# Batch 5's 1/rms spread over the partitions by a round trip through DRAM, with a new order of the whole work

## The chip, the core and the metric

The kernel runs on one core of a Trainium2 chip. The metric is the time of one execution on the device in microseconds (us), the median of several runs. The core has five engines, each with its own queue of instructions in a fixed order: TensorE (PE, matmuls, results into PSUM), VectorE (DVE), ScalarE (ACT), GpSimd (POOL) and SyncE (SP). Here GpSimd only issues loads, and SyncE only issues transfers. An instruction that must wait holds up all that is behind it on its engine.

## The reference

```python
# attention: q, k, v are [8 batches, 8 heads, 576, 64]
kv  = einsum('bhsd,bhse->bhde', k, v)
out = einsum('bhsd,bhde->bhse', q, kv)
rms = sqrt(mean(out * out, axis=-1, keepdims=True) + 1e-06)
x   = out / rms * g_norm            # then heads side by side: [8, 576, 512]
# channel mix: w_k [512, 1024], w_v [1024, 512], w_r [512, 512]
x_prev = x shifted by one position, zero first
xk = mu_k * x + (1 - mu_k) * x_prev
xr = mu_r * x + (1 - mu_r) * x_prev
y  = sigmoid(xr @ w_r) * (max(xk @ w_k, 0) ** 2 @ w_v)
```

All inputs and the output are fp32; the kernel computes in bf16 with fp32 sums.

## The kernel before

The attention part goes batch by batch (0 to 7), with channels on the partitions: four pairs of heads of 128 channels each, 576 positions along the free axis. The channel mix goes over nine groups g of 512 positions, across the borders of the batches.

The code defines *pieces* with names, and a string, ORDER, lists all of them by hand. `Plan.run` (L95) walks the string and issues each piece at that place. A token is a name, then the engine if there is a choice (A ScalarE, D VectorE, S SyncE), then the numbers of the buffers that the piece takes: `K5.3::2` takes PSUM slot 2. There are four PSUM slots (`ps`), four output buffers (`out`), two each of k, v, q, qT, uT, xT, and one `sq`. A piece that takes a slot waits on the chip until the last user of that slot is done. So ORDER sets every queue, and the slots set many of the waits.

The pieces of batch b, with their lines:

- `load_kB`, `load_vB`, `load_qB`: loads that turn fp32 into bf16, issued by GpSimd (L280); weights at L264.
- `kv` (L353, L368 for batches 0 and 1): k times v on TensorE, copied out by `kvc` or `kvm`.
- `qT`: q transposed on TensorE (L406, L411, batches 0 to 2), or `qTd` (L394), a transposing transfer on SyncE (batches 3 to 7).
- `u` (L430, L436): q times kv; `uc` copies it to uT, `sq` squares it.
- `st` (L526): sums of squares, all four pairs at once, on TensorE. `rs` (L531): 1/rms on ScalarE, 16 equal rows per head.
- Then 1/rms has to reach all 64 channels of a head. For batches under SPREAD (L145) `sp` (L565, two halves of four matmuls) spreads it into two PSUM slots, and four multiplies `x` (L570) read it there. For the others `rw` (L541) writes one row per head to DRAM, `rr` (L545) reads it back 64 times over into the `sq` buffer, and two multiplies `x` (L550) read that. Batch 0 has its own way (`ss`, `rs`, `x`, L488 to L497).
- `d` (L591): x minus the position before; `tk`, `tr` (L190 or L192): times mu; `xk`, `xr` (L601): the two blends.

The pieces of group g: `K` (L636, eight of them), `relu` (L640) and `sqk` (L643) square the result, `R` (L658) and `sig` (L663) give the gate, `V` (L692) is the second matmul in halves a and b, `o` (L696) multiplies it with the gate into an output buffer, and `S` (L622) stores it, two transfers each. `idle:n` (L742) issues n matmuls on zeros. ScalarE loads a table for 1/sqrt (L204) or sigmoid (at L663) when it goes from one to the other.

In the old order SyncE's queue around the change is: qTd5, S2.0, S2.1, S0.1, S0.0, qTd6, S2.2, S1.3, S2.3, S1.2, qTd7, S3.0, S3.2, rw6, S3.1, rr6, rw7, S4.1, S3.3, rr7, S4.2 and the other stores. ScalarE issues only some of the last stores. o5.1 takes the output buffer that S3.2 and S3.3 store from, and R6.1 the PSUM slot that o5.1 reads.

Of the kernel before, what the change touches and what calls it, by code (L numbers as in the profile page):

```python
# [12 lines left out]


ORDER = """
    zero load_q1.0::0 early_k::0 early_v::1 ident ident9 ones load_v0.6::0 load_q0.6::1 cast_k:D:0 mu_k_load:A load_q0.2
    idle:52:0 qT0.1::0 qT0.3::1 cast_v:A qTc0.3:D:0 load_k0.6 kv0.3::2 qT1.0::3 kv0.0::1 qTc1.0:A:1 kvm0.3::0 kvm0.0 load_q0.0
    qT0.0::2 g_load mu_r_load:S load_q0.4 load_v0.2 sel_load load_k0.4 load_k0.2 mu_mm::3 qT0.2::1 qTc0.0:D qTc0.1:A u0.0::2
    sq0.0::0 u0.3::0 sq0.3 load_v0.4 sel mu uc0.3:A:0 uc0.0:D idle:5:3 ss0.0::3 qTc0.2:A rs0.0::0 kv0.2::2 kv0.1::0 kvm0.2
    kvm0.1 ss0.3::1 u0.2::2 u0.1::0 uc0.2:D load_v1.4::1 load_k1.4::1 load_q1.4 qT1.1::3 load_v1.0 load_k1.0 rs0.3::1 load_w_r0  # L20
    qTc1.1:D x0.0::0 sq0.1 sq0.2 idle:13:1 ss0.2::1 rs0.2::0 ss0.1::3 d0.0::0 tk0.0:D:0 x0.3 d0.3 uc0.1:A rs0.1::1 load_w_r1
    kv1.2::2 idle:2:1 qT1.2::1 kvm1.2::1 qTc1.2:A idle:13:0 u1.2::0 uc1.2:A:1 qT1.3::3 load_w_k0 qTc1.3:A x0.1 tr0.0:D:1 x0.2
    d0.2 d0.1 xr0.0 tr0.1:D tk0.1:D tr0.2:A xr0.2 xr0.1 tk0.2:A idle:9:1 kv1.0::2 tr0.3:D kvm1.0 u1.3::1 uc1.3:A tk0.3:A
    idle:2:0 R0.0::03 R0.1 xr0.3 xk0.0 xk0.1 xk0.3 u1.0::1 uc1.0:D load_w_k1 R0.2 R0.3.1 u1.1::2 sig0.1::0 R0.3.0 sig0.0::1
# [12 lines left out]
    sp3.1::01 V2.1b x3.1.1::1 sp3.0::21 V2.0b x3.1.0 x3.0.0 x3.0.1 V2.2a::0 S0.2 S1.1 S0.3 S1.0 u4.2::21 d3.0::0 d3.2 tk3.0:D:1
    xk3.0 tk3.2:D xk3.2 V2.3a V2.3b uc4.3:A:0 uc4.2:A u4.0::12 sq4.1:A:0 uc4.0:A uc4.1:A V2.2b load_v6.0::1 load_k6.0::0 o2.0::3
    tr3.2:A:0 xr3.2 kv6.0::1 tr3.0:D o2.1::1 K3.3::2 K3.2 kvc6.0.2:A:1 K3.1::3 K3.0 load_k5.0::1 load_v5.0::0 kvc6.0.1:A sq4.0:A
    relu3.1::0 kvc6.0.0:A load_q5.0::1 qTd5::1 st4::0 rs4::0 S2.0 S2.1 S0.1 relu3.0::1 K3.6::2 sp4.0::10 sqk3.1::1 K3.7  # L40
    relu3.3::0 x4.0.1::0 x4.0.0 K3.5::3 load_k7.0::0 kv5.0::0 S0.0 sqk3.0 xr3.0 sp4.1::12 K3.4 x4.1.1 x4.1.0 sqk3.3 relu3.2::1
    sqk3.2 kvc5.0.1:D:0 d4.0::0 R3.3::2 R3.1::1 R3.0 V3.1a::3 V3.1b R3.2 V3.0a V3.0b d4.2 tk4.2:D:1 kvc5.0.0:A kvc5.0.2:A
    tr4.2:A:0 sig3.0::1 tk4.0:D xk4.2 xk4.0 sig3.1::2 load_q7.0::0 K4.6::0 K4.4::1 K4.7 tr4.0:D relu4.3::0 xr4.2 xr4.0 K4.2::2
    K4.5 relu4.2::1 load_q6.0::1 qTd6::0 sqk4.3::0 K4.3 K4.1::0 K4.0 o3.0::3 sqk4.2 relu4.0::0 relu4.1::1 R4.2::1 V3.2a::3 R4.3
    u5.2::02 V3.3a V3.2b sig4.1::0 uc5.2:A:1 uc5.3:D sq5.1:A:0 sqk4.1 sqk4.0 u5.0::12 uc5.0:A V3.3b R4.1::0 uc5.1:D sq5.0:D
    o3.1::2 st5::1 R4.0 rs5::1 sp5.1::23 V4.3a::1 V4.2a x5.1.0::1 x5.1.1 sig4.0::1 load_v7.0::1 sp5.0::23 kv7.0::0 x5.0.1
    d5.2::0 x5.0.0 d5.0 tk5.0:D:1 S2.2 S1.3 S2.3 S1.2 kvc7.0.1:A:0 kvc7.0.2:A tk5.2:A kvc7.0.0:A qTd7::1 V4.2b V4.1a::3 V4.0a
    V4.3b xk5.0 o4.1::1 xk5.2 u6.0::20 V4.0b tr5.0:A:0 uc6.1:A:0 uc6.0:A sq6.0:A:0 S3.0 S3.2 V4.1b u6.2::01 K5.3::2 K5.2 uc6.3:A
    uc6.2:D sq6.1:D st6::1 rs6::0 K5.1::0 relu5.1::1 K5.6::1 K5.7 K5.0 relu5.0::0 tr5.2:D xr5.2 xr5.0 sqk5.1::1 relu5.3::1
    K5.5::2 K5.4 sqk5.0 relu5.2::0 o4.0::0 R5.0::0 R5.1 R5.3::1 V5.3a::2 R5.2 sig5.0::2 sig5.1::0 sqk5.2 sqk5.3 u7.2::30 rw6:S  # L50
    S3.1 rr6:S x6.0::0 x6.1 uc7.2:A:1 uc7.3:A V5.2a V5.3b u7.0::13 V5.1a::0 V5.0a d6.0::0 V5.0b V5.1b V5.2b uc7.1:A sq7.1:A:0
    uc7.0:A sq7.0:A st7::3 rs7::1 rw7:S S4.1 S3.3 rr7:S S4.2 S4.0 d6.2 tk6.0:D:1 tk6.2:D xk6.2 xk6.0 K6.3::1 K6.2 K6.0::3 K6.1
    tr6.2:A:0 relu6.1::0 o5.0::3 tr6.0:D K6.5::0 K6.4 xr6.2 xr6.0 sqk6.1::0 o5.1::2 S5.3 S5.2 relu6.0::1 sqk6.0 K6.6::1 K6.7
    R6.3::3 R6.1::2 relu6.2::0 relu6.3::1 sqk6.3 sqk6.2 R6.0 V6.2a::0 V6.0a::1 V6.0b V6.3a V6.3b R6.2 S5.0 x7.0::1 V6.1a V6.1b
    V6.2b d7.0::0 x7.1 d7.2 tk7.2:D:1 tk7.0:D xk7.0 xk7.2 sig6.1::1 tr7.2:D:0 sig6.0::2 K8.1::3 o6.0::0 o6.1::2 K8.3::2 K8.0
    tr7.0:A relu8.0::1 sqk8.0::1 K8.2 K8.4::1 relu8.1::0 K8.5 K8.6::0 K8.7 S4.3 S6.0 sqk8.1 xr7.2 relu8.2::1 relu8.3::0 sqk8.2
    sqk8.3 V8.3.0a::3 K7.2::2 K7.1::1 K7.3 V8.3.0b K7.0 S6.2 relu7.1::1 K7.4::0 relu7.0::0 K7.6::2 K7.5 K7.7 sqk7.0::0 xr7.0
    relu7.2::0 R8.2::1 R8.3 sqk7.2 relu7.3::0 sig8.1::0 sqk7.1 o8.1.3.0::1 sqk7.3 R7.0::0 R7.1 V8.2a::2 R7.3::1 sig7.0::2 R7.2
    V8.2b V7.2a::3 V7.2b V7.1a::0 o8.1.2.0 S6.3 S8.3.3.0.b:S S8.3.3.0.a:S S5.1 S6.1 S8.2.2.0.a:S sig7.1::1 V7.1b V7.3a V7.3b
    o7.1::2 S7.2.a:A S7.3.a:A R8.1::1 V7.0a V7.0b o7.0::3 V8.1a::2 R8.0 V8.1b S7.3.b:S S7.2.b:A S7.1.a:A V8.0a::3 V8.0b S7.1.b:S  # L60
# [56 lines left out]
def kernel(  # L117
# [15 lines left out]
    B, H, S, HD = q.shape  # L133
# [8 lines left out]
    G = 512  # L142
    NG = B * S // G
    DMA_T = 3
    SPREAD = 6  # L145
    BLOCK = (0,1,)
    DIRECT = ()
    PARTS = {0: ((0, 1), (1, 1), (2, 1), (3, 1)), 1: ((0, 2), (2, 2))}
# [25 lines left out]
             for tag, (n, shape, dt) in BUFS.items() for i in range(n)}  # L174
    scratch = {b: dram.tile([H, S], BF16, name=f"scratch{b}") for b in range(SPREAD, B)}
    plan = Plan()
# [40 lines left out]
    ones = const.tile([128, 2, HD], BF16, name="ones")  # L217
# [3 lines left out]
    sel = const.tile([128, 2, HD], BF16, name="sel")  # L221
# [108 lines left out]
    def attention(b):  # L330
# [183 lines left out]
        else:  # L514
# [21 lines left out]
            xms = {hp: [] for hp in range(NHP)}  # L536
            if b >= SPREAD:
                rows8 = scratch[b]
# [16 lines left out]
                for i in range(2):  # L555
# [219 lines left out]
```

## Time and profile before

| | us |
|---|---|
| median of 9 runs | 207.81 |
| lowest and highest | 206.04, 209.33 |
| the profiled execution | 207.22 |
| its span | 205.2 |

| what, in the profiled execution | start, us |
|---|---|
| first R0 matmul | 23.62 |
| st5, rs5 | 117.50, 117.98 |
| sp5.1, sp5.0 | 118.83, 120.89 |
| x5.1.0 (first x5 multiply), last xk5 ended | 119.16, 127.77 |
| first K5 | 128.13 |
| last V8 matmul ended | 200.52 |

The span runs from the first to the last instruction of the program; the execution's own time has 2.0 us around it. In what follows a line of the profile has the engine, the line of the code, the operation and the tiles (out<-in), and times in us from the start of the span. "x40" counts instructions. In the rows of groups there follow busy time, mean ns of one, and the idle time in front of them with what ended it. In a timeline the first two numbers are start and duration, and a bracket at the end names the idle time before.

### The profile page before, as it was taken

To read this page: it belongs to the slowest core of one execution; us is meant where nothing else is said; L and a number is where in the kernel's file an instruction comes from. 1 tells how busy PE (TensorE), PEld (TensorE's weight loads), DVE (VectorE), ACT (ScalarE), POOL (GpSimd) and SP (SyncE) were. 2 spreads that over 40 slices of the span, in tenths; PEclk is the share of its full clock that TensorE was granted. 3 is DMA by queue.
4 is the path that set the end of the run, shared out by engine and by line. 5 is a ranking of instruction groups with operands and counts; after the bars stand their busy time and mean duration, and the time that the engine had idled before them with its cause. 6 is when DMAs were issued, how large, how long until landed. Compare 5 with 4: busy or idle time off the path is not lost.

```text
span 205.2 us, 3907 instructions
## 1 busy us (share of the span) xinstructions
PE 196.8 (96%) x1578; PEld 98.6 (48%) x1578; DVE 140.2 (68%) x253; ACT 123.0 (60%) x151; POOL 29.7 (14%) x46
## 2 busy tenths in 40 slices
PE   7879999999999999999999999999998999999990
PEld 6858644464344534435476344443443434444440
DVE  3149975999599688989964778869736996241241
ACT  2177877377834586794575879687974256363010
POOL 7984530004000114020200000000000000000000
PEclk9999999999999999999999999999999999999997
DMA  6999999999999599999899991060057414005074
GB/s 156 195 199 202 207 205 205 204 203 204 203 187 216 162 127 132 202 203 177 188 203 218 237 180 40 22 149 0 0 160 242 129 27 127 0 5 143 10 230 128
DMA packets 40437, 30.91 MB, mean 151 GB/s; under 512 B 13644, under 2 KB 35940, under 8 KB 40420
## 3 DMA queue, kind: packets, MB, share of 16 engines
q0 software_dynamic: 21248, 16.48, 52.7%
q1 hardware_dynamic: 18444, 13.14, 26.9%
q10 hardware_dynamic: 728, 1.05, 1.7%
q8 instruction: 12, 0.20, 0.4%
q14 instruction: 5, 0.04, 0.1%
HBM read 34.74 MB, written 9.46 MB: 215 GB/s over the span
## 4 chain that ended last, share of the span: by engine, by line
PE 82%; DMA 5%; DVE 4%; POOL 3%; ACT 2%; issue 1%; SPq 1%; DVEq 0%; POOLq 0%
PE ps L692 29%; PE ps L636 27%; PE ps L658 13%; DMA v<-in_v_dram 3%; PE ps L353 3%; PE ps L436 2%; DMA out_dram<-out 2%; PE ps L742 2%; PE ps L526 1%; POOL q L280 1%; PE ps L565 1%; PE ps L368 1%; POOL k L280 1%; DVE out L696 1%; PE ps L430 1%
## 5 line engine op out<-in xcount | busy, mean ns | idle before, releaser
L692 PE MATMUL ps<-w_v,sqk 128*128 128x512 bf16 (+1 forms) x296 | 67.2, 374 | 0.0
L636 PE MATMUL ps<-xk,w_k 128*128 128x512 bf16 (+1 forms) x320 | 66.0, 358 | 0.3 <-DVE xk L601 0.2
L640 ACT ACTIVATE relu<-ps 128x1024 bf16<-128x1024 f32 x36 | 36.0, 1022 | 28.8 <-PE ps L636 24.1
L636 PEld LDWEIGHTS <-w_k 128*128 128x128 bf16 x320 | 30.1, 98 | 30.9 <-issue 2.3
L692 PEld LDWEIGHTS <-sqk 128*128 128x128 bf16 x296 | 27.7, 98 | 32.9 <-issue 1.8
L643 DVE TENSOR_TENSOR sqk<-relu 128x1024 bf16<-128x1024 bf16 x36 | 24.3, 688 | 20.9 <-ACT relu L640 20.9
L658 PE MATMUL ps<-w_r,xr 128*128 128x512 bf16 x144 | 35.2, 379 | 0.5 <-DVE out L696 0.5
L696 DVE TENSOR_TENSOR out<-ps,sig 128x1024 f32<-128x1024 f32 (+2 forms) x21 | 22.2, 1068 | 16.5 <-PE ps L692 9.5
L663 ACT ACTIVATE sig<-ps 128x1024 bf16<-128x1024 f32 x18 | 18.1, 1022 | 18.5 <-DMA out_dram<-out 9.4
L658 PEld LDWEIGHTS <-xr 128*128 128x128 bf16 x144 | 13.6, 98 | 16.3 <-issue 2.0
L190 ACT ACTIVATE t<-d,mu_sb 128x576 bf16<-128x576 bf16 x23 | 16.5, 770 | 7.5 <-DVE d L591 7.4
L570 DVE TENSOR_TENSOR xT<-uT,ps 128x576 bf16<-128x576 bf16 x20 | 14.2, 750 | 3.3 <-PE ps L565 3.1
L192 DVE TENSOR_SCALAR t<-d,mu_sb 128x576 bf16<-128x576 bf16 x41 | 13.8, 382 | 0.2
L742 PE MATMUL ps<-zeros 128*128 128x224 bf16 x96 | 12.2, 287 | 1.2 <-DVE zeros L231 1.2
L280 POOL DMA_DIRECT2D q<-in_q_dram x12 | 8.6, 720 | 30.4 <-PE ps L411 16.2
L591 DVE TENSOR_TENSOR d<-xT 128x1152 bf16<-128x1152 bf16 (+1 forms) x18 | 12.4, 691 | 0.6
L601 DVE TENSOR_TENSOR xr<-t,xT 128x1152 bf16<-128x1152 bf16 (+1 forms) x18 | 11.8, 684 | 1.5 <-ACT t L190 1.4
L186 DVE CAST uT<-ps 128x576 bf16<-128x576 f32 x12 | 8.8, 753 | 5.5 <-PE ps L436 5.3
L184 ACT CAST uT<-ps 128x576 bf16<-128x576 f32 x16 | 9.8, 636 | 4.5 <-PE ps L436 3.6
L601 DVE TENSOR_TENSOR xk<-t,xT 128x1152 bf16<-128x1152 bf16 (+1 forms) x18 | 11.8, 685 | 0.2
L280 POOL DMA_DIRECT2D v<-in_v_dram x11 | 7.9, 716 | 23.7 <-PE ps L353 22.3
L742 PEld LDWEIGHTS <-zeros 128*128 128x128 bf16 x96 | 9.9, 109 | 2.3 <-DVE zeros L231 1.2
(61 smaller groups left out, 135.5 us busy)
## 6 DMA issues: line engine op xcount, KB each, us to landing
out_dram<-out SPq DMA_DIRECT2D x21, 192.0 KB
v<-in_v_dram POOLq DMA_DIRECT2D x6, 576.0 KB, 10.7
q<-in_q_dram POOLq DMA_DIRECT2D x6, 576.0 KB, 10.5
k<-in_k_dram POOLq DMA_DIRECT2D x6, 576.0 KB, 11.4
out_dram<-out SPq DMA_DIRECT2D x23, 128.0 KB
out_dram<-out SPq DMA_DIRECT2D x21, 64.0 KB
sq<-scratch SPq DMA_DIRECT2D x4, 288.0 KB
w_k<-in_moe_w_k_dram POOLq DMA_DIRECT2D x2, 512.0 KB, 13.0
```

The source lines that it names most:

```text
L190: nc.scalar.mul(out=dst, in_=src, mul=by)
L280: nc.gpsimd.dma_start(out=get(kvq[(n, b)])[:, h0:h1, :], in_=rows(n, b, h0, h1))
L570: nc.vector.tensor_tensor(out=get(xT)[:, 2 * i:2 * i + 2, NP + c:NP + c + HS], in0=flat(slice(2 * i, 2 * i + 2))[:, :, c:c + HS], in1=get( ...
L601: nc.vector.tensor_tensor(out=dst[:, hsl, c0:c0 + S], in0=get(t[key])[:, hsl, :], in1=get(xT)[:, hsl, 0:S], op=ALU.add)
L636: nc.tensor.matmul(get(ps)[:, fc % 2, a0:a1], w_k_sb[:, cc, 128 * fc:128 * fc + 128], xk[:, cc, x0:x0 + a1 - a0], start=(cc == 0), stop=(c ...
L640: nc.scalar.activation(out=get(rt), in_=get(ps), func=AF.Relu)
L643: nc.vector.tensor_mul(out=get(sqk)[:, 2 * f2:2 * f2 + 2, :], in0=get(rt), in1=get(rt))
L658: nc.tensor.matmul(get(ps)[:, ci % 2, :], xr[:, cc, c:c + 128], w_r_sb[:, cc, :], start=(cc == 0), stop=(cc == NHP - 1))
L663: nc.scalar.activation(out=get(sg), in_=get(ps), func=AF.Sigmoid)
L692: nc.tensor.matmul(get(ps)[:, ci % 2, cs], get(sqk)[:, fc, 128 * ci:128 * ci + 128], w_v_sb[:, fc, cs], start=(fc == 0), stop=(fc == NFC - 1))
L696: nc.vector.tensor_mul(out=get(ot)[:, xs, cs], in0=get(ps)[:, xs, cs], in1=get(sg)[:, xs, cs])
L742: nc.tensor.matmul(tiles[("ps", slot)][:, 0, HS:512], zeros[:, 0:128], zeros[:, HS:512], start=True, stop=True)
```

## The change

SPREAD goes from 6 to 5, so that batch 5 takes the way of batches 6 and 7: `sp5.0`, `sp5.1` and four x5 multiplies go, `rw5`, `rr5` and two multiplies come. ORDER is written anew from its first token to its last: places, engines and slots of nearly all pieces differ.

```diff
 ORDER = """
-    zero load_q1.0::0 early_k::0 early_v::1 ident ident9 ones load_v0.6::0 load_q0.6::1 cast_k:D:0 mu_k_load:A load_q0.2
-    idle:52:0 qT0.1::0 qT0.3::1 cast_v:A qTc0.3:D:0 load_k0.6 kv0.3::2 qT1.0::3 kv0.0::1 qTc1.0:A:1 kvm0.3::0 kvm0.0 load_q0.0
...
-    o3.1::2 st5::1 R4.0 rs5::1 sp5.1::23 V4.3a::1 V4.2a x5.1.0::1 x5.1.1 sig4.0::1 load_v7.0::1 sp5.0::23 kv7.0::0 x5.0.1
-    d5.2::0 x5.0.0 d5.0 tk5.0:D:1 S2.2 S1.3 S2.3 S1.2 kvc7.0.1:A:0 kvc7.0.2:A tk5.2:A kvc7.0.0:A qTd7::1 V4.2b V4.1a::3 V4.0a
...
-    K5.5::2 K5.4 sqk5.0 relu5.2::0 o4.0::0 R5.0::0 R5.1 R5.3::1 V5.3a::2 R5.2 sig5.0::2 sig5.1::0 sqk5.2 sqk5.3 u7.2::30 rw6:S
-    S3.1 rr6:S x6.0::0 x6.1 uc7.2:A:1 uc7.3:A V5.2a V5.3b u7.0::13 V5.1a::0 V5.0a d6.0::0 V5.0b V5.1b V5.2b uc7.1:A sq7.1:A:0
-    uc7.0:A sq7.0:A st7::3 rs7::1 rw7:S S4.1 S3.3 rr7:S S4.2 S4.0 d6.2 tk6.0:D:1 tk6.2:D xk6.2 xk6.0 K6.3::1 K6.2 K6.0::3 K6.1
...
+    zero load_v0.2::0 load_k0.2::0 idle:31:0 kv0.1::0 ones mu_k_load:S early_k::0 load_q0.4::0 g_load load_q0.2 load_k0.4
+    load_v0.4 load_q1.4::1 load_k1.4::1 ident load_q0.0 ident9 idle:1:1 qT0.2::1 early_v::1 mu_r_load:A mu_mm::2 qT0.1::3
...
+    uc1.2:A sq1.1:A:0 idle:5:3 qT1.0::3 qT1.1::1 qTc1.1:A qTc1.0:D xr0.1 load_w_v0 idle:4:0 u1.0::2 R0.0::03 u1.1::1 d0.3
+    tk0.3:D xk0.0 xk0.1 tr0.3:A xr0.3 R0.1 R0.2 R0.3.0 uc1.0:A uc1.1:A sq1.0:D load_w_v1 sig0.0::0 R0.3.1 st1::2 sig0.1::1
...
+    kv4.0::3 st3::1 R2.3 kvc4.0.0:D:0 kvc4.0.2:D kvc4.0.1:D rs3::0 sp3.0::21 V2.1a::3 V2.1b x3.0.0::1 x3.0.1 sp3.1::21 sig2.1::2
...
+    K3.0::1 K3.1 relu3.1::1 sp4.1::32 sqk3.2::1 x4.1.1 x4.1.0 d4.0::0 sqk3.1 d4.2 tk4.2:D:1 R3.2::0 R3.3 qTd5::1 qTd6::0 K3.7::2
+    K3.6 R3.1::3 R3.0 S2.1 relu3.0::0 sig3.1::0 tk4.0:A xk4.0 xk4.2 S1.1 S1.0 sig3.0::1 relu3.3::1 kv5.0::1 kv6.0::0
...
+    V3.3a::0 K4.4 V3.3b V3.2a V3.2b rw5:S xr4.2 S2.0 o3.1::2 R4.2::3 R4.3 relu4.2::0 u6.2::21 sig4.1::2 R4.1::0 R4.0 sqk4.2
+    sqk4.3 uc6.2:D:0 uc6.3:D rr5:S V4.1a::3 V4.1b u6.0::21 sig4.0::1 S3.0 S2.3 S1.3 S3.1 qTd7::1 S2.2 x5.0::1 kv7.0::0 x5.1
+    uc6.0:A uc6.1:A kvc7.0.1:A:0 d5.0::0 V4.0a V4.2a::2 V4.0b V4.3a V4.2b sq6.0:A:0 sq6.1:A st6::1 rs6::1 rw6:A d5.2 tk5.0:D:1
...
+    rr6:A tr5.2:D xr5.0 xr5.2 sqk5.0::1 K5.5::3 K5.6::2 K5.7 K5.3 relu5.1::1 sqk5.1 relu5.3::0 R5.0::1 K5.4 R5.2::0 R5.3 R5.1
...
+    rs7::0 rw7:S S4.1 S4.0 rr7:S K6.3 relu6.1::0 K6.7::0 K6.6 tr6.0:D:0 o5.1::0 xr6.0 tr6.2:D xr6.2 sqk6.1::0 K6.1::2 K6.0
...
+    V8.0a::0 V8.0b o8.0.0.0::2 S8.0.0.0.a:S S7.1.a:A S8.0.0.0.b:S V8.1a::1 V8.1b o8.0.1.0 S8.1.1.0.a:A S8.1.1.0.b:S
 """
...
-    SPREAD = 6
+    SPREAD = 5
```

What the prediction speaks of in it:

- *Start.* The loads begin with pair 1 of batch 0 and end with pair 3; the same loads of batches 0 and 1 still stand ahead of the first weights (`load_w_r0`). `ident` is issued by GpSimd after eight loads. The zero matmuls are 82 instead of 96, the first stretch 31 instead of 52. u1.0 stands before R0, and st1 right before the first K0.
- *SyncE's queue.* qTd3, S0.0, qTd4, S0.1, S0.3, S0.2, qTd5, qTd6, S2.1, S1.1, S1.0, rw5, S2.0, rr5, S3.0, S2.3, S1.3, S3.1, qTd7, S2.2, S3.2, S4.3, S1.2, S3.3, rw7, S4.1, S4.0, rr7 and the other stores. rw6 and rr6 are issued by ScalarE.
- *Output buffers.* o3.0 takes the one that S1.0 and S1.1 store from, o3.1 that of S2.0 and S2.1, o4.1 that of S2.2 and S2.3, o5.1 that of S1.2 and S1.3, o5.0 that of S3.2 and S3.3.
- *ScalarE's tables.* Between the sigmoids sig2.0 and sig2.1 stands rs3, and rs4 after them, so that the tables change 16 times instead of 14.
- *Tail.* The last pieces are V8.1, o8.0.1.0 (128x512) and its two stores, in place of the half-width V8.3.1, o8.1.3.1.

## The prediction

> **What bounds the kernel now.** I read the page first, then its chain, the waits, and the engines' timelines around each wait.
>
> ```profile
> span 205.2 us, 3907 instructions
> ...
> PE 196.8 (96%) x1578; PEld 98.6 (48%) x1578; DVE 140.2 (68%) x253; ACT 123.0 (60%) x151; POOL 29.7 (14%) x46
> ...
> PEclk9999999999999999999999999999999999999997
> ...
> PE 82%; DMA 5%; DVE 4%; POOL 3%; ACT 2%; issue 1%; SPq 1%; DVEq 0%; POOLq 0%
> ```
>
> TensorE is busy for 96% of the span at a full clock and makes 82% of the chain. From the first R0 matmul (23.62 us) to the last V8 matmul (end 200.52) it has almost no gap, so what the change takes from its queue there counts one to one. Before 23.62 the loads set the pace: w_r0, which R0 needs, lands at 23.26. After 200.52 come 4.6 us of eviction and store.
>
> I laid the old order's pieces from 23.62 end to end, at the start-to-start times that the timeline shows for their kinds (K, R, V 0.86 us; kv of a batch 0.88; u 0.37; st 0.36; 0.10 more where K, R or V gives way to a small piece). That ends at 198.26; the real end is 200.52, so 2.26 us are waits. The largest, 0.69 us, shows in the waits and in the timelines of VectorE, TensorE and SyncE:
>
> ```profile
> DVE out L696 <- DMA out_dram<-out: 3.0, 1, 3.0
> ```
>
> ```profile
> 154.48 1.23 DVE L696 TENSOR_TENSOR out<-ps,sig 128x1024 f32<-128x1024 f32 x1 [3.04 <-DMA out_dram<-out]
> ```
>
> ```profile
> 155.76 1.89 PE L658 MATMUL ps<-w_r,xr 128*128 128x512 bf16 x8 [0.53 <-DVE out L696]
> ```
>
> ```profile
> 148.08 0.61 SPq L541 DMA_DIRECT2D scratch<-rs  x1
> 148.79 1.80 SPq L622 DMA_DIRECT2D out_dram<-out  x4
> 151.19 2.49 SPq L545 DMA_DIRECT2D sq<-scratch  x2
> ```
>
> SyncE had stood at rw7 (L541) until rs7 came at 148.05; S4.1 and S3.3 were queued behind it. S3.3 went out at 149.7-150.6 and landed at 154.40 (the semaphore's update), o5.1 needed its output slot and began at 154.48, and R6.1, which needs o5.1's PSUM slot, stood. So a wait on SyncE in front of stores is how the round trip can cost TensorE.
>
> **The change part by part.**
>
> *Removed:* sp5.0 and sp5.1, eight of the matmuls of L565. The groups of instructions (count, busy time, mean ns of one, idle time before them):
>
> ```profile
> L570 DVE TENSOR_TENSOR xT<-uT,ps 128x576 bf16<-128x576 bf16 x20 | 14.2, 750 | 3.3 <-PE ps L565 3.1
> ...
> L204 ACT ACT_TABLE_LOAD x7 | 9.0, 1283 | 0.8 <-PEq L759 0.7
> ...
> L550 DVE SCALAR_TENSOR_TENSOR xT<-uT,mu_sb,sq 128x1152 bf16<-128x1152 bf16 x4 | 5.6, 1414 | 0.2 <-DMA sq<-scratch 0.2
> ...
> L565 PE MATMUL ps<-rs,sel 32*128 32x288 bf16 x40 | 3.0, 291 | 0.0
> ```
>
> Each sp holds TensorE 0.23 us (118.83 to 119.06, 120.89 to 121.12) and the step into it 0.10: 2 x 0.33 = **-0.66 us** on the path. VectorE: four x5 multiplies of 0.750 (3.00) become two of 1.414 (2.83): -0.17, not on the path.
>
> *Added: the round trip of batch 5.* rw5 (9 KB), then rr5 (two of 288 KB), on SyncE. From batch 6: rw6 issued at 131.12 landed at 132.84 (1.72); rr6 issued from 133.13, landed at 137.13 and 138.29 (5.16). In the new order st5 stands at about 110.3 on TensorE (its place laid end to end, 109.6, plus the waits below), rs5 ends near 111.4, rw5 issues to 112, S2.0 to 113.1, rr5 from 113.2, landed by 118.4. VectorE reaches x5.0 at about 119 (it has o3.1, two sqk, two uc before it), so the trip is hidden by 0.6 us. After x5.0 come x5.1, two d, two tk, two xk: 7.3 us to K5.0, which TensorE reaches at 127.5; so TensorE has 1.2 us more. The round trip also keeps the one sq buffer until x5.1 ends (121.8); sq6.0 wants it at 122.6. Cost **0**; without the cover each us of lateness past 1.8 is paid.
> Behind rw5's wait on SyncE stand S2.0, rr5, S3.0, S2.3, S1.3, S3.1, qTd7 and S2.2. o3.1 waits for S2.0: issued 112-113.1, landing after 2.4 (the quiet row: S2.2 at 112.04 took 2.51) near 115.0, just when V3.2b ends (115.2). qTd7 and S2.2 serve u7 (140) and o4.1 (128.5): free.
>
> *Moved: rw6/rr6 to ScalarE, and S3.3 ahead of rw7.* o5.1 now takes the slot of S1.2 and S1.3, out near 129, and o5.0 that of S3.2 and S3.3, out near 138, before SyncE comes to rw7 (148). So the 0.69 wait goes: **-0.69 us**. rw6 and rr6 cost ScalarE about 1.9 us of issue in a stretch where relu5.0 and relu5.1 are 3 us apart: 0. Behind rw7 now stand S4.1, S4.0, rr7; rr7 lands near 156.5 and x7.0 is reached at 156.9, in front of K8 by its 6.8 us of chain (163.7 against 163.6): a wait of 0.1-0.2 where before had 0.32.
>
> *Moved: the start.* The first work is now pair 1, pair 3 comes last; the same loads still stand ahead of w_r0, so it lands at 23.3 again. Adding the durations by dependence, R0.0 comes out at 23.6. Fourteen fewer zero matmuls (21 fewer of the first 52, 7 more later) only fill such waits: 0. u1.0 moves ahead of R0 (-0.25), but st1 now stands before K0 and ScalarE has 11.5 us of work between 15.3 and 26.4 up to uc1.1, then table load, sig0.0, sig0.1, table load, rs1, relu0.0 to 32.6, where sp1.0 wants it at 32.3: +0.3, and K0.0 about 0.15 late. Net **+0.2**, between -0.2 and +1.5.
>
> *Moved: one more switch of ScalarE's tables.* rs3 and rs4 now stand around sig2.1: 16 loads instead of 14. The row: 1.283 us each, and in the timeline the sigmoid starts 0.01 us after its load (103.21, 103.22). At the row's price rs3 ends at 77.95 and sp3.0, due at 77.8, waits **+0.15**. The Trainium skill (ScalarE: Activation LUTs, What ACT_TABLE_LOAD costs) puts a drain of 1.38 us on top, 2.66 per switch; the two loads ahead of rs3 would then make it 2.8 us later and cost about 2.9 us. This trace has no such drain, so I take the row.
>
> *Moved: S1.1 and S1.0 behind qTd5 and qTd6.* This is the open cost. SyncE's timeline before:
>
> ```profile
> 92.26 5.42 SPq L394 DMA_TRANSPOSE qT<-q  x1
> 97.78 5.81 SPq L622 DMA_DIRECT2D out_dram<-out  x8
> 107.70 4.24 SPq L394 DMA_TRANSPOSE qT<-q  x1
> ```
>
> q5 should land near 91.3 in the new order (v5, k5, k6, q5 issue from 76.6, when kv4 ends; the first lands 5.9 later, each next 2.9), so the transposes hold SyncE to about 101 (5.4 + 4.2) and S2.1, S1.1, S1.0 go out at 101-104.3. o3.0 needs S1.0's slot: it is due at 109.1 and TensorE starts to wait if it begins after 109.5 (V3.3a). S1.0's last half issues at about 103.9-105.2, while q7, v7 and k7 load. Quiet stores land after 2.1-2.5 us, those issued at 101.2-103.1 beside two loads took 6.5-6.9: landing between 106.3 and 111.9, a wait of **0 to 2.4 us**. [...]Three transfers are 8.7 us of load from about 101.5 and the stores 2.5 us; at half a share the stores are through near 108-109. I take 0.1.
>
> *Moved: the tail.* The last eviction is 128x512 (0.69 us) instead of 128x256 (0.42), its stores twice as large: 0.27 + 0.13 = **+0.4**.
>
> *Sum* on the profiled execution (207.22: span 205.2 and 2.0 around it): -0.66 - 0.69 + 0.2 + 0.15 - 0.1 (K8) + 0.1 + 0.4 = -0.6; the smaller waits that the old order had and I find no counterpart for (0.31 before K4.4, 0.24 after K8.1) make it **-1.1**: 206.1. The median is 0.59 above that execution, so **206.7** against 207.81.
>
> **The rivals.**
> *Even.* The small waits that I can't see in a new order are as many as in the old one, and the start is a little late: -1.1 + 0.55 + 0.3 = -0.25, 207.5. For it: VectorE and ScalarE were 9 tenths busy in several slices, and every engine's order is new. Against: nothing single.
> *Slower: S1.0 late.* If S1.0 lands at 111.9, o3.0 starts 2.4 us after its deadline, V3.3a stands, and VectorE's queue (tr4, sqk4.1, xr4, o3.1) with it: -1.1 - 0.1 + 2.4 = +1.2, 209.0. It decides from a landing of about 111.7. For it: the 6.5 us rows, and three loads instead of two. Against: fewer stores queued (768 KB, not 1 MB), and the loads may be done earlier.
> *The round trip takes sp5's place as a wait.* rr7 needed 6.3 us beside stores, not 5.16: landing 119.5, 1.3 us before TensorE feels it. 0.5 more would cost 0.5: 207.2. Small.
> *Much faster.* The start gains its 0.25 and waits fall to 1.3 in all: -2.5, 205.3.
>
> **How the numbers follow.** A difference of 0.5% (1.04 us) is about what a measurement of this kernel can tell from none. The forecast and the much faster case hold 0.41; even and the round-trip case 0.28; slower 0.31, since a late start or the table's drain adds to S1.0. Predicted is the likeliest case, 206.7, with its own range 205.4-206.8; the range over all, a tenth left out at either end, is 204.8 to 209.6.
>
> **What would show it.** Right: L565 x32, L550 x6, ACT_TABLE_LOAD x16 in all; rr5 landing before VectorE is free for x5.0; no wait of L696 for a store near 150; R0 at 23.3-24.0; first K5 within 0.3 us after V4.3b. Wrong: L696 waiting for out_dram<-out near 109-112 with TensorE standing at L692; K8 or K5 waiting on L601; R0 after 24.5; an idle ScalarE of over 1 us behind a table load.

## The result

The changed kernel takes **205.76 us** in the median of 16 executions (204.80 to 208.82), beside 208.03 for the kernel before (206.04 to 210.93, 53 executions): a ratio of **0.9903**, 95% interval 0.9876 to 0.9929, so 1.0% faster. The ratio leaves out the executions that took over 1.5% more than the fastest of their kernel, so it is not the quotient of the medians. Forecast were 206.7 and "faster", with 204.8 to 209.6 as the range.

In the execution that was profiled first (208.82 us) TensorE's clock fell to half near the start (the 7 and the 5 in its PEclk row), so the start is read from a second profile of the same kernel (after_again), 205.94 us long. The page of the first, then of the second:

```profile
span 207.0 us, 3871 instructions
...
PE 197.8 (96%) x1556; PEld 99.2 (48%) x1556; DVE 140.5 (68%) x257; ACT 123.4 (60%) x147; POOL 29.6 (14%) x46
...
PEclk9759999999999999999999999999999999999998
```

```profile
span 204.1 us, 3871 instructions
...
PE 195.2 (96%) x1556; PEld 97.4 (48%) x1556; DVE 140.5 (69%) x257; ACT 123.4 (60%) x147; POOL 29.4 (14%) x46
...
PEclk9999999999999999999999999999999999999997
```

The span of the second is 1.0 us below that of before (204.12 and 205.16). TensorE is still busy for 96% of it and still the bound. The groups of instructions in that second profile (count, busy time, mean ns of one, idle time before them):

```profile
L204 ACT ACT_TABLE_LOAD x8 | 10.3, 1283 | 0.9 <-PEq L759 0.7
L663 ACT ACT_TABLE_LOAD x8 | 10.3, 1283 | 0.1
...
L550 DVE SCALAR_TENSOR_TENSOR xT<-uT,mu_sb,sq 128x1152 bf16<-128x1152 bf16 x6 | 8.3, 1411 | 0.0
...
L565 PE MATMUL ps<-rs,sel 32*128 32x288 bf16 x32 | 2.5, 291 | 0.1
```

Eight matmuls of L565 are gone, two multiplies of L550 came, and there are 16 table loads. L550 waited for nothing, so no round trip was late for VectorE in this execution.

The place of the largest old wait, first VectorE's timeline, then SyncE's, of the first profile:

```profile
151.25 1.22 DVE L696 TENSOR_TENSOR out<-ps,sig 128x1024 f32<-128x1024 f32 x1
```

```profile
114.74 0.63 SPq L541 DMA_DIRECT2D scratch<-rs  x1
115.42 0.89 SPq L622 DMA_DIRECT2D out_dram<-out  x2
117.87 1.36 SPq L545 DMA_DIRECT2D sq<-scratch  x2
...
152.07 0.60 SPq L541 DMA_DIRECT2D scratch<-rs  x1
```

o5.1 (L696 at 151.25) begins with no wait for a store (no bracket behind its line), and rw7 (152.07) comes after it. The 3.04 us that VectorE stood there before, and the 0.69 us of TensorE behind it, are gone.

One wait has come in: TensorE stands 1.0 us longer than the pieces need in the first profile, 0.28 us in the second. The second profile's waits, its VectorE and its TensorE:

```profile
DVE out L696 <- DMA out_dram<-out: 0.6, 1, 0.6
```

```profile
109.22 0.75 DVE L198 TENSOR_TENSOR sq<-uT 128x1152 bf16<-128x1152 bf16 x1
110.56 1.23 DVE L696 TENSOR_TENSOR out<-ps,sig 128x1024 f32<-128x1024 f32 x1 [0.59 <-DMA out_dram<-out]
```

```profile
111.20 0.43 PE L526 MATMUL ps<-sq,ones 128*32 128x288 bf16 x8
111.84 1.02 PE L692 MATMUL ps<-w_v,sqk 128*128 128x512 bf16 x4 [0.21 <-DVE out L696]
```

o3.0 wanted the buffer of S1.0 and S1.1, and V3.3a (111.84) wanted the PSUM slot of o3.0. In the first profile S1.0 was issued at 105.17 to 106.36 and landed at 113.36; o3.0 began at 113.48, and TensorE stood for 0.93 us by the trace. This is a place that the forecast had named as a sign of its being wrong; the other that came true is R0 after 24.5 (24.75 in the second profile).

Against the old profile, the second one divides like this. The pieces laid end to end, as in the forecast, end at 197.35 instead of 198.26 if both start at 23.62.

| | before | after_again | difference |
|---|---|---|---|
| R0.0 begins | 23.62 | 24.75 | +1.13 |
| pieces from R0.0 on, end to end | 174.64 | 173.73 | -0.91 |
| waits among them | 2.26 | 1.11 | -1.15 |
| after the last V8 matmul | 4.64 | 4.53 | -0.11 |
| span | 205.16 | 204.12 | -1.04 |

The waits of after_again: 0.12 within sp1.0 (in front of K0.5), 0.20 at sp3.0, 0.28 at V3.3a, 0.12 at K8.2, the rest under 0.06 each. Of the 0.91, 0.66 are the two sp and 0.25 is u1.0, now ahead of R0.0. In medians the difference in that comparison is larger, 205.72 against 207.21; the old kernel's executions scatter more than the new one's, which the last experiment takes up. L550 waited for nothing here, but in two later profiles of the same order (with 52 and with 12 zero matmuls) VectorE stood 0.21 and 0.44 us at x5.0 for rr5; TensorE did not wait at K5 in any of the four.

### The profile page after: what moved, and what is told of

It reads as the page before. It is cut to its first block, busy times and chain, and to the rows that moved or that the text cites. A ratio compares the mean times of both kernels' runs of the same rounds, so it can differ in the third digit from the quotient of the medians.

```text
span 207.0 us, 3871 instructions
## 1 busy us (share of the span) xinstructions
PE 197.8 (96%) x1556; PEld 99.2 (48%) x1556; DVE 140.5 (68%) x257; ACT 123.4 (60%) x147; POOL 29.6 (14%) x46
## 3 DMA queue, kind: packets, MB, share of 16 engines
q10 hardware_dynamic: 1304, 1.72, 3.2%
## 4 chain that ended last, share of the span: by engine, by line
PE 82%; DMA 6%; DVE 3%; ACT 2%; issue 2%; SPq 2%; POOL 0%; DVEq 0%; POOLq 0%
PE ps L692 29%; PE ps L636 28%; PE ps L658 13%; DMA out_dram<-out 4%; DMA k<-in_k_dram 3%; PE ps L742 2%; PE ps L353 2%; PE ps L436 2%; PE ps L368 2%; SPq L622 1%; PE ps L565 1%; PE ps L406 1%; DVE out L696 1%; PE ps L430 1%; PE ps L526 1%
## 5 line engine op out<-in xcount | busy, mean ns | idle before, releaser
L692 PE MATMUL ps<-w_v,sqk 128*128 128x512 bf16 (+1 forms) x296 | 66.9, 374 | 0.9 <-DVE out L696 0.9
L692 PEld LDWEIGHTS <-sqk 128*128 128x128 bf16 x296 | 28.0, 98 | 33.3 <-issue 2.5
L696 DVE TENSOR_TENSOR out<-ps,sig 128x1024 f32<-128x1024 f32 (+2 forms) x21 | 22.1, 1068 | 15.7 <-PE ps L692 9.7
L184 ACT CAST uT<-ps 128x576 bf16<-128x576 f32 x18 | 11.0, 639 | 7.0 <-PE ps L436 6.9
L192 DVE TENSOR_SCALAR t<-d,mu_sb 128x576 bf16<-128x576 bf16 x41 | 13.3, 368 | 0.2
L570 DVE TENSOR_TENSOR xT<-uT,ps 128x576 bf16<-128x576 bf16 x16 | 11.3, 748 | 1.1 <-PE ps L565 1.1
L186 DVE CAST uT<-ps 128x576 bf16<-128x576 f32 x10 | 7.4, 753 | 5.3 <-PE ps L436 5.3
```

What stands on the lines that cost most here:

```text
L192: nc.vector.tensor_scalar_mul(out=dst, in0=src, scalar1=by)
L692: nc.tensor.matmul(get(ps)[:, ci % 2, cs], get(sqk)[:, fc, 128 * ci:128 * ci + 128], w_v_sb[:, fc, cs], start=(fc == 0), stop=(fc == NFC - 1))
L696: nc.vector.tensor_mul(out=get(ot)[:, xs, cs], in0=get(ps)[:, xs, cs], in1=get(sg)[:, xs, cs])
```

## Experiments

The orders below are shown as the tokens that were moved. A line number of a kernel whose order has become two lines longer is two higher than in the kernel before (L698 for L696).

### The same kernel once more

No edit: the changed kernel as it is.

> The changed kernel unaltered, for a second profile and more times. In its first profile TensorE's clock was at half from 7.9 to 14.8 us and R0 began at 26.94 us. If that is an event of single executions, most executions do without it: span 203.0 to 204.3 us, median 205.5 to 206, R0 at 23.3 to 24.0 us, and a wait of 0.5 to 1.5 us of TensorE at V3.3a behind o3.0, which waits for the stores S1.0 and S1.1. Rival: the half clock belongs to every execution and the gain lies elsewhere; then R0 is again near 27 us.

Measured: 205.72 us (205.09 to 206.91), 0.9932 of the kernel before, interval 0.9903 to 0.9962. R0.0 began at 24.75, 2.2 us before that of the first profile, and V3.3a waited 0.28 us instead of 1.0. Its median lies in the expected 205.5 to 206, R0.0 a little behind the expected 23.3 to 24.0, and the wait at V3.3a below the expected 0.5 to 1.5. So the late start of the first profile, over 2 us, is an event of single executions, and the wait at V3.3a belongs to the change, with a size that varies.

### More and fewer zero matmuls at the start

```diff
- zero load_v0.2::0 load_k0.2::0 idle:31:0 kv0.1::0
+ zero load_v0.2::0 load_k0.2::0 idle:52:0 kv0.1::0
```

> The first stretch of zero matmuls is 52 again instead of 31, so that TensorE is busy until 7.9 us, when the first data are there, instead of 5.9. If the idle 2 us are what lets the clock fall, no execution has it at half in the start, the slow ones (above 206.5 us) go, and the median is 0 to 0.5 us under the unaltered kernel. Rival: the fallen clock has nothing to do with this stretch; then the spread of the times stays, and the median is the same or up to 0.1 us later.

```diff
- zero load_v0.2::0 load_k0.2::0 idle:31:0 kv0.1::0
+ zero load_v0.2::0 load_k0.2::0 idle:12:0 kv0.1::0
```

> The changed kernel with 12 zero matmuls in the first stretch instead of 31, so that TensorE stands from about 3.4 us until the first data at 6.5 to 7.9. If idle time there leaves or brings the clock to half, most executions now have it at half until 12 us or later, and R0 comes 1 to 3.5 us later (median 206.7 to 209). Rival: the loads set R0 whatever the clock does in the start; then the median stays within 0.4 us of the unaltered changed kernel (205.7).

With 52: 206.15 us (0.9964, 0.9938 to 0.9990), no better than the 205.72 of 31. With 12: **208.84 us** (1.0031, 0.9997 to 1.0066), by the medians 3.1 us more than with 31, by the ratios to the kernel before (0.9932 with 31) 2.0. TensorE's timeline with 12, and then that of the first profile with 31:

```profile
2.66 0.95 PE L742 MATMUL ps<-zeros 128*128 128x224 bf16 x4
6.37 0.85 PE L368 MATMUL ps<-v,k 96*64 96x128 bf16 x12 [2.76 <-DMA k<-in_k_dram]
...
12.62 0.45 PE L488 MATMUL ps<-sq,ones 128*128 128x288 bf16 x2
...
25.43 1.03 PE L658 MATMUL ps<-w_r,xr 128*128 128x512 bf16 x3
```

```profile
7.90 0.84 PE L368 MATMUL ps<-v,k 96*64 96x128 bf16 x12 [1.95 <-DMA k<-in_k_dram]
...
14.14 0.69 PE L488 MATMUL ps<-sq,ones 128*128 128x288 bf16 x2
14.62 0.49 PE L430 MATMUL ps<-qT,kv 128*128 128x288 bf16 x2
```

The column after the start is the length. In the first profile of the changed kernel the granted clock is half from 7.9 to 14.8, and R0.0 began at 26.94; a pair of L488 takes 0.69 us there and 0.45 or less at full clock. With 12 zero matmuls the twelve of L368 take 0.85 us at 6.37, as at half clock in the first profile (0.84), and the pair of L488 at 12.62 is the first piece at full length: TensorE is still at half clock until 12.7. (The trace's first record of a full clock is at 12.70 there and at 3.9 to 6.8 in the other profiles; the PEclk row shows nines before a first record too.) This profile is of the mildest execution (206.37 us; the others reach 210.84), and its R0.0 is at 25.43, only 0.7 us behind that of after_again; the 2 to 3 us of the others stand in no profile. So the zero matmuls are not only filling of waits: with too few of them TensorE is slow for longer at the start, and the kernel takes 2 to 3 us more. With 31, 26 of 28 executions stay under 207 us. Whether 52 would have prevented the fall in the first profile stays open, since every execution of that kernel and of after_again had a mean clock of 0.994 or more. That 52 do not always prevent it is seen in the old order further down.

### S1.1 and S1.0 back ahead of the transposes

```diff
- R3.2::0 R3.3 qTd5::1 qTd6::0 K3.7::2 K3.6 R3.1::3 R3.0 S2.1 ... xk4.2 S1.1 S1.0 sig3.0::1
+ R3.2::0 R3.3 S1.1 S1.0 qTd5::1 qTd6::0 K3.7::2 K3.6 R3.1::3 R3.0 S2.1 ... xk4.2 sig3.0::1
```

> S1.1 and S1.0 stand before qTd5 on SyncE instead of behind qTd6. If o3.0's wait for them is what holds V3.3a, L696 no longer waits for out_dram<-out near 110 us, the wait at V3.3a goes, and the kernel is 0.8 to 1.2 us faster than the unaltered one (ratio 0.985 against the kernel before). Rival: the time is given back at the next wait (o3.1 for S2.0, or x5 for rr5), or the transposes come later behind the stores; then within 0.3 us of the unaltered one.

Measured: **204.96 us** (204.70 to 205.24), 0.9909 (0.9883 to 0.9936), 0.76 us below the changed kernel beside it; a later repetition, in the next part, gave 204.89. SyncE, VectorE and TensorE of this kernel:

```profile
67.20 5.05 SPq L624 DMA_DIRECT2D out_dram<-out  x8
92.29 7.80 SPq L396 DMA_TRANSPOSE qT<-q  x2
```

```profile
108.55 0.75 DVE L200 TENSOR_TENSOR sq<-uT 128x1152 bf16<-128x1152 bf16 x1
109.22 1.22 DVE L698 TENSOR_TENSOR out<-ps,sig 128x1024 f32<-128x1024 f32 x1
```

```profile
110.53 0.43 PE L528 MATMUL ps<-sq,ones 128*32 128x288 bf16 x8
110.89 1.04 PE L694 MATMUL ps<-w_v,sqk 128*128 128x512 bf16 x4
```

The expectation was 0.8 to 1.2 us. SyncE issues S1.1 and S1.0 by 72.3 (the last four of the eight at 67.20), the last lands at 79.5, o3.0 begins at 109.22 behind its neighbour, and V3.3a stands right behind st5. The cause of the new wait is shown: the stores behind two transposes. Its size is not one number: 0.28 and 1.0 us in two profiles of the changed kernel, 0.58 in that with 52 zero matmuls, none in that with 12. Of the 0.9 us between the spans of this profile and after_again's (203.2 and 204.1), 0.67 are an earlier R0.0 (24.08), which the edit does not touch, so the 0.76 of the medians is an estimate of the wait with that uncertainty.

### Batch 5 spread by TensorE again, in the new order

First the new order with SPREAD at 6 again and the eight matmuls put back where there was room:

```diff
- V3.3b V3.2a V3.2b rw5:S xr4.2 S2.0 ... uc6.3:D rr5:S V4.1a::3 ... S2.2 x5.0::1 kv7.0::0 x5.1
+ V3.3b sp5.0::32 x5.0.0::1 x5.0.1 V3.2a V3.2b xr4.2 sp5.1::32 x5.1.0 x5.1.1 S2.0 ... uc6.3:D V4.1a::3 ... S2.2 kv7.0::0
```

> The new order, but batch 5 spread by TensorE again: sp5.0 and sp5.1 among V3's matmuls, four multiplies, no rw5 and rr5. If the round trip of batch 5 is hidden and saves TensorE's 0.66 us, this is 0.5 to 0.9 us slower than the unaltered changed kernel and still about 1.3 us faster than the kernel before. Rival: the gain is all the round trip's, then it is as slow as the kernel before (+2 us); or the round trip costs as much in waits as it saves, then no difference.

Measured: 208.48 us (1.0075, 1.0045 to 1.0105), 2.76 above the changed kernel beside it, not 0.5 to 0.9. Its VectorE, TensorE and SyncE say why:

```profile
111.54 1.23 DVE L698 TENSOR_TENSOR out<-ps,sig 128x1024 f32<-128x1024 f32 x1 [2.23 <-DMA out_dram<-out]
...
115.85 1.42 DVE L572 TENSOR_TENSOR xT<-uT,ps 128x576 bf16<-128x576 bf16 x2 [1.93 <-PE ps L567]
117.19 0.75 DVE L603 TENSOR_TENSOR xr<-t,xT 128x1152 bf16<-128x1152 bf16 x1
```

```profile
112.82 1.02 PE L694 MATMUL ps<-w_v,sqk 128*128 128x512 bf16 x4 [1.85 <-DVE out L698]
```

```profile
99.93 17.23 SPq L624 DMA_DIRECT2D out_dram<-out  x16
```

Without rw5 there is no wait in SyncE's queue that holds back S2.0; it goes out at 103.87, right behind S1.0, and S1.0 lands at 111.42 instead of 110.44, with R0.0 0.66 us earlier: TensorE stands 1.9 us at V3.3a. That S2.0 beside it makes S1.0 land later is likely and not shown, since this wait varies without it too. The x5.0 multiplies (L572) stand ahead of xr4.2 (L603) on VectorE, which costs 0.9 us at R4.2. So this run measures two other waits besides the matmuls, and says little on the round trip. The next pair takes both away: S1.1 and S1.0 early in both kernels, and in the second sp5.0 earlier, behind K4.4, and sp5.1 with its multiplies behind xr4.2.

```diff
- V3.3a::0 K4.4 V3.3b V3.2a V3.2b rw5:S xr4.2 ... relu4.2::0 u6.2::21 sig4.1::2 ... sqk4.3 uc6.2:D:0 uc6.3:D rr5:S ... x5.0::1 ... x5.1
+ V3.3a::0 K4.4 sp5.0::32 V3.3b V3.2a V3.2b x5.0.0::1 x5.0.1 xr4.2 ... relu4.2::0 sp5.1::12 sig4.1::2 ... sqk4.3 x5.1.0 x5.1.1 u6.2::21 uc6.2:D:0 uc6.3:D
```

> Like the kernel with S1.1 and S1.0 before qTd5, but batch 5 spread by TensorE again (sp5.0 after K4.4, sp5.1 after R4.3, u6.2 behind R4.0), without the late stores that fell on after_sp5. If the round trip's own part is TensorE's 0.66 us and little else, this is 0.5 to 1.0 us slower than after_s1_early (205.5 to 206.0 us). Rival: the round trip brings more than that, as after_sp5 seems to say; then 1.5 us or more (206.5 and up), without a wait of V3.3a for stores.

Measured: 206.12 us (0.9927, 0.9900 to 0.9955), 1.16 above the 204.96 of after_s1_early and so a little over the expected 1.0. The two had not been measured side by side; here they are:

> The changed kernel with S1.1 and S1.0 ahead of qTd5, once more, so that it stands beside the next kernel in one call. Measured earlier 204.96 (0.9909 of the kernel before): 204.7 to 205.3 again.

> The same order with batch 5 spread by TensorE (eight matmuls in two pieces, the two DMA steps gone). If the round trip of batch 5 saves what its matmuls cost, 2 x 0.33 us, and adds no wait, this is 0.66 us slower than the kernel beside it, up to 1.1 with the small waits that the earlier profile showed at u6.2. If the round trip had cost a hidden wait of its own, the difference would be under 0.4. Earlier, across two calls, the difference was 1.16 us of time and 0.94 at TensorE's last matmul.

Measured: **204.89 us** (0.9911, 0.9876 to 0.9945) with the round trip, **206.07 us** (0.9966, 0.9943 to 0.9988) with the matmuls: 1.18 us for the round trip of batch 5 in an order that gives it room. By the ratios the first is 1.8 us faster than the kernel before and the second 0.7, so in this order (S1.1 and S1.0 early) the round trip is the larger part of the gain and the moves are the smaller. The kernel with the matmuls has again the 40 of the kernel before (group of its first run):

```profile
L565 PE MATMUL ps<-rs,sel 32*128 32x288 bf16 x40 | 3.2, 290 | 0.1
```

TensorE's last matmul ends at 198.81 and 199.76 in these two profiles, 0.95 apart: 0.66 for the two pieces, 0.07 at R0.0, and about 0.2 in small waits such as 0.14 at u6.2 in the first run. Another 0.2 lies after the last matmul (4.51 and 4.70 us), all of it behind the landing of the last store, where no piece is left, so it is no part of the round trip. The 0.66 is there, the difference is just over the expected 1.1, and the rival of a hidden wait, which wanted less than 0.4, falls.

### The round trip in the old order

```diff
- o3.1::2 st5::1 R4.0 rs5::1 sp5.1::23 V4.3a::1 V4.2a x5.1.0::1 x5.1.1 ... sp5.0::23 kv7.0::0 x5.0.1 d5.2::0 x5.0.0 d5.0 tk5.0:D:1 S2.2 S1.3 S2.3 S1.2
+ o3.1::2 S2.2 S1.3 S2.3 S1.2 st5::1 R4.0 rs5::1 rw5:S rr5:S V4.3a::1 V4.2a ... kv7.0::0 x5.1::1 d5.2::0 x5.0 d5.0 tk5.0:D:1
...
- SPREAD = 6
+ SPREAD = 5
```

> The kernel before with the round trip of batch 5 alone: SPREAD 5, rw5 and rr5 right after rs5, the four stores of o1.1 and o2.1 in front of them, everything else in the old order. rs5 ends at 118.6, rw5 lands 1.7 us later, rr5 5.2 us after that, so x5 starts at 125.5 instead of 119.2 us, and the first K5 at 132.5 to 133 instead of 128.1: 3.5 to 4.5 us slower than before (ratio 1.019), TensorE standing before K5 or V4. Rival: the old order has enough slack behind st5 (V4 is there), then within 1 us of the kernel before.

Besides the round trip itself, four stores were moved ahead of it.

Measured: **212.89 us** (1.0251, 1.0210 to 1.0293), 5.2 us slower than the kernel before, where 3.5 to 4.5 were expected. Its clock row, waits, SyncE, ScalarE and TensorE:

```profile
PEclk9999999999999999999999996699999999999999
```

```profile
DVE xT L550 <- DMA sq<-scratch: 8.2, 2, 7.4
```

```profile
119.00 0.64 SPq L541 DMA_DIRECT2D scratch<-rs  x1
120.89 1.36 SPq L545 DMA_DIRECT2D sq<-scratch  x2
```

```profile
128.74 1.44 ACT L190 ACTIVATE t<-d,mu_sb 128x576 bf16<-128x576 bf16 x2 [5.65 <-DVE d L591]
130.20 0.37 ACT L184 CAST kv<-ps 128x256 bf16<-128x256 f32 x1
```

```profile
125.80 0.32 PE L436 MATMUL ps<-qT,kv 64*64 64x288 bf16 x4
130.62 0.46 PE L436 MATMUL ps<-qT,kv 64*64 64x288 bf16 x4 [4.51 <-ACT kv L184]
131.01 3.60 PE L692 MATMUL ps<-w_v,sqk 128*128 128x512 bf16 x8
```

rs5 ends at 119.0, rw5 lands at 120.75, the data of rr5 are there at 126.1: VectorE stands for 7.4 us. The trip itself takes 7.1 us; in the new order it took 7.0 (after_s1_early), 7.2 (after_again) and 8.2 (first profile). What stops TensorE is not K5 but a smaller thing: tk5.2 waits on ScalarE for d5, a kv copy is queued behind it (130.20), and u6.0 needs the PSUM slot of that copy. TensorE stands 4.5 us. While it stands its clock falls to half, from 128.4 to 135.2, and the eight matmuls of L692 at 131.01 take 3.60 us in place of 1.89, so by this estimate about 1.7 us of the 5.2 come from the clock and not from the wait. So the transfer takes as long in both orders; what the change brings is that in its order other work lies over it.

### S3.3 ahead of rw7, in the old order alone

```diff
- st7::3 rs7::1 rw7:S S4.1 S3.3 rr7:S S4.2 S4.0
+ st7::3 rs7::1 S3.3 rw7:S S4.1 rr7:S S4.2 S4.0
```

> The kernel before with one store moved: S3.3 before rw7 on SyncE. If the 0.69 us at R6.1 come from S3.3 standing behind rw7's wait, L696 no longer waits for out_dram<-out near 151 to 154 us, R6.1 follows R6.3 at once and the kernel is 0.5 to 0.8 us faster than before (ratio 0.997). Rival: the wait at K8 for x7 takes the place of the one removed, so that nothing or 0.1 us is gained.

> The kernel before with S3.3 put ahead of rw7, once more, since the first verdict was unclear (7 of 12 executions at a granted clock of 0.979 to 0.987). Theory: the wait of 0.69 us at R6.1 is gone and about as much comes back, up to 1.0 with what followed it: ratio 0.995 to 0.997 in executions at a full clock. Rival: the wait only moves on to the next eviction, ratio 1.000.

First run: 208.16 us (1.0016, 0.9974 to 1.0058), unclear, since 7 of its 12 executions had a mean clock of 0.979 to 0.987. Second run: **206.32 us** (0.9971, 0.9940 to 1.0002). VectorE's timeline of the first:

```profile
150.97 0.68 DVE L643 TENSOR_TENSOR sqk<-relu 128x1024 bf16<-128x1024 bf16 x1
151.58 1.22 DVE L696 TENSOR_TENSOR out<-ps,sig 128x1024 f32<-128x1024 f32 x1
```

o5.1 begins at 151.58 without a wait; before it was 154.48. From R0.0 to the last V8 matmul TensorE takes 175.66 us instead of 176.90, so 1.24 of the 2.26 us of waits are gone: the 0.69 at R6.1, and with it the two at K8 (0.32 and 0.24). Nothing took their place. By time the ratio is 0.6 us below one, and its interval just touches one. The mechanism is shown by the trace, its size in time is likely but not sure. A further sign: in the second run the ten executions with a mean clock of 0.994 and more lie between 205.89 and 206.36, while those of the kernel before at 0.994 and more scatter from 205.85 to 208.32. The kernel without the wait at V3.3a scatters little too (after_s1_early, 204.70 to 205.24), the one with it more (after_again, 205.09 to 206.91). So a wait of TensorE for a store goes with scattered times; that it makes them so is not shown.

The profile of the second run fell on an execution of 210.33 us, with its clock row

```profile
PEclk9955999999999999999999999999999999999997
```

and R0.0 at 27.91. It is the old order with its 52 zero matmuls, and the clock falls at the start all the same. The number of zero matmuls alone does not decide on that fall, and what does is not settled here.

## Why the prediction was right

The sign and most of the mechanisms held, and the time fell into the likeliest case's own range. That the sum agrees to a tenth is luck: the start came 0.8 us worse than forecast, the tail 0.5 and the waits 0.2 better.

- **sp5 removed, -0.66.** Right: it is in the laid-out pieces of the new order, and the matmuls put back cost at least that.
- **The round trip hidden, cost 0.** Right, with less room than expected in the unlucky case. In after_again rw5 landed 2.06 us after its issue and the last of rr5 5.0 us after its own, at 119.77; x5.0 began at 120.03, without a wait, and K5.0 at 128.81 right behind V4.3b (127.94). In the first profile rw5 took 3.0 us: the load of k7 was in flight beside it until 117.27. rr5 landed at 122.92, x5.0 began at 123.03, and K5.0 (131.73) was still not late. The margin at VectorE, 0.6 in the forecast, was 0.26 in after_again, 0.1 here, and gone in the two profiles where VectorE stood 0.21 and 0.44 us, so it was the slack counted at TensorE behind it that kept the cost at 0. That the old order without the moves costs 5.2 us shows what the cover is worth, the fallen clock included.
- **S3.3 no longer behind rw7, -0.69.** Right, and too small: no wait of L696 near 150, and the same move alone in the old order takes 1.24 us of waits away, since those at K8 go with it.
- **The start, +0.2.** Wrong in size: this is the term that failed most. R0.0 was forecast at 23.6 and begins at 24.08 to 24.82 in the seven profiles of the new start with an undisturbed clock and 31 or 52 zero matmuls, against 23.62 to 23.97 in three of the old. In after_again w_r0 landed at 24.23 instead of the forecast 23.3, and u1.0, which stands before R0.0, waited for ScalarE until 24.49. In the seven profiles w_r0 landed at 23.53 to 24.23. GpSimd's timeline before, then in after_again:

```profile
12.71 1.45 POOL L264 DMA_DIRECT2D w_r<-in_moe_w_r_dram  x2 [0.17 <-issue]
```

```profile
11.86 0.67 POOL L280 DMA_DIRECT2D k<-in_k_dram  x1 [0.83 <-DMA q<-in_q_dram]
13.26 0.67 POOL L280 DMA_DIRECT2D q<-in_q_dram  x1 [0.74 <-DMA k<-in_k_dram]
14.00 0.71 POOL L264 DMA_DIRECT2D w_r<-in_moe_w_r_dram  x1
```

  The same loads do stand ahead of w_r0, but in the new order GpSimd had to wait for earlier ones to land in front of two of them, so it issued w_r0 1.3 us later. The forecast had looked at which loads come first and not at when GpSimd may issue them. The load alone does not set R0.0: with 52 zero matmuls it landed at 23.53, and R0.0 began at 24.82, behind a u1.0 that waited for VectorE. How the two divide was not tried. The other half of this step, sp1.0 +0.3 and K0.0 +0.15, measured 0.12. "Fewer zero matmuls: 0" held from 52 to 31, and would not have held at 12.
- **One more table switch, +0.15.** Right: sp3.0 waited 0.20. ScalarE's timeline in after_again:

```profile
76.90 1.28 ACT L204 ACT_TABLE_LOAD   x1
78.19 0.65 ACT L531 ACTIVATE rs<-ps 128x576 bf16<-128x576 f32 x1
```

  A load of 1.28 us and the next function 0.01 after it. The drain of 1.38 us that the Trainium skill (ScalarE: Activation LUTs, What ACT_TABLE_LOAD costs) adds would have given 2.9 us here; the row was the better price.
- **S1.0 behind qTd5 and qTd6, 0.1 taken of 0 to 2.4.** The mechanism was named, its size was too low: 0.28 and 1.0 us in two profiles, 0.76 in the medians. S1.0 landed at 110.44 in after_again, 85.7 us after R0.0, and 86.4 after it in the first profile; the forecast had the stores through near 108-109, with half a share beside the loads. The halves of S1.0 are 128 KB each, not 192. They took 7.1 to 7.7 us from issue to landing in these two profiles, three times the 2.4 to 2.5 of quiet ones, so half a share was too much.
- **Smaller waits, -0.5, and K8, -0.1.** Right or too small: K8.2 waited 0.12 instead of 0.32, and the 0.24 after it is gone.
- **The tail, +0.4.** Wrong: 4.53 and 4.51 us after the last V8 matmul against 4.64, -0.1. The last eviction is 0.27 us longer, as forecast (0.69 for 0.42), but what follows it, forecast 0.13 longer, takes 3.8 us in after_again and took 4.2 before. Twice the bytes in the last stores did not show: the last one (192 KB, issued at 200.36) landed after 2.24 us, that of before (96 KB, issued at 201.01) after 2.49, with two more stores issued 0.6 us ahead of it. That these held it up is likely and was not tried. The remaining 0.1 lies behind the landing of the last store.

With the measured terms the sum reads: start +1.1, pieces -0.9, waits -1.15, tail -0.1, so -1.0 in the span, and the forecast had said -1.1. The waits fell by nearly what S3.3's move takes away in the old order; the new ones (0.20 at sp3.0, 0.28 at V3.3a, 0.12 at sp1.0) and the other old ones that went about cancel. The rival "even" failed because the waits of the new order are fewer, not as many. The rival "slower" had the right place and stayed 1.4 us short of its price. "Much faster", 205.3, lies nearer to the measured 205.76 than the forecast's 206.7 does, but not for its reason: the start lost where it should have gained. Its -2.5 does not follow from its terms either, which give about -1.5 (-0.66 for sp5, -0.96 for waits down to 1.3, -0.25 for the start, +0.4 for the tail).

The medians differ by 1.5 and 2.3 us in the two comparisons and not by 1.1. The two profiled executions differ by 1.28 (207.22 and 205.94), 0.2 more than their spans. The rest is where the medians lie: 205.72 is 0.2 below the profiled execution of after_again, and in the result's comparison 208.03 is 0.81 above that of before, not the 0.59 carried over. No profile here divides these parts further.

## What to carry to other kernels

A round trip through DRAM is bought with the order and not with its own time: list what lies over it on every engine, then what is queued behind its waits, down to the small copy behind a late activation. A store whose buffer is wanted back belongs ahead of long transposes and loads in its queue, and when a wait on SyncE in the middle of a queue is removed, look at which stores it had been keeping apart. Price the start and the end of a kernel from their own chains, as carefully as its middle, down to when each load can be issued; here the two largest errors lay there.

## What the runs showed of the hardware

- A store of 128 KB took 2.4 to 2.5 us from issue to landing on quiet queues (before, issued at 112.04 to 113.91) and 7.1 to 8.2 us beside three loads of 576 KB (S1.0 in the first profile, after_again and after_sp5).
- rw5, a write of 9 KB to DRAM beside the load of k7 (576 KB), took longer the longer that load still had to run: 1.72 us with 1.7 us to go (after_s1_early), 2.06 with 2.0 (after_again), 2.6 to 3.1 with 2.3 to 2.7 (the first profile and those with 12 and 52 zero matmuls). With no load beside it it took 1.76 (before_rt5). The two reads of 288 KB behind it took 5.0 to 5.3.
- TensorE's granted clock was half for 6.8 us (7.9 to 14.8) in the first profile of the changed kernel, where TensorE had stood 1.95 us just before, and for 10.2 us (11.2 to 21.4) in before_s33_early_2, where no gap between its first matmul and the fall was longer than 0.7 us. R0.0 came 2 to 4 us later in these two than in other executions of the same order. It was half again for 6.8 us in before_rt5, beginning 2.3 us into a stand of 4.5 us.
